# A transformer block on one core: modulation rows summed on VectorE, and part of the modulation moved to ScalarE

## The chip, the cores and the metric

The kernel runs on one core of one Trainium2 chip. The metric is the device time of one execution in microseconds. A core has five engines that run their own instruction queues in order and wait for one another on semaphores: TensorE (PE in the profile; its weight loads are listed as PEld), VectorE (DVE), ScalarE (ACT), GpSimd (POOL) and SyncE (SP), which here only issues DMAs. Before the change the median of three runs is 848.65 us (848.63 to 848.72).

## The reference

One block with a linear attention part and a gated feed-forward part, both steered by a condition vector `c`. Sequence length S = 2048, width D = 1024, hidden width F = 3584, 32 heads of 32 columns, bf16 inputs and output.

```python
mod = (silu(c) @ w_mod).reshape(1, 6, 1, -1)       # w_mod: 1024 x 6144
sa, ca, ga, sb, cb, gb = mod[:, 0], ..., mod[:, 5]  # six rows of 1024
h = layernorm(x) * (1 + ca) + sa
q, k, v = h @ wqkv
pq, pk = phi(q), phi(k)                             # phi(t) = where(t > 0, t + 1, exp(t)) + 1e-6
kv = sum over s of pk * v;  z = sum over s of pk    # per head
o = (pq @ kv) / (pq . z + 1e-6)
x = x + ga * (o @ wo)
h = layernorm(x) * (1 + cb) + sb
x = x + gb * ((silu(h @ w_gate) * (h @ w_up)) @ w_down)
```

The six rows of `mod` are vector-matrix products of length 1024. The rows sa and ca are needed at the start. The other four, ga, sb, cb and gb, are the "late" rows: ga scales the columns of the attention output, sb and cb shift and scale the second normalised input, gb scales the columns of the last product.

## The kernel before

**Tiles and stages.** The 2048 rows are 16 row tiles of 128, in four chunks of 512. `M4` holds h transposed, [128 partitions, chunk, 8 column blocks, 512 rows], so that a column block's sa, ca are one number per partition. The schedule is by hand: `seq` is a list of labelled pieces of TensorE work, and `put(label, ...)` hangs further work behind a label. The program is issued piece by piece in that order, and each engine keeps the order in which its instructions are issued.

The stages are, in order: K and V of chunk 0; then per chunk sc the stage KV (partial sums of kv, in banks 5 to 7 of PSUM, two halves of 16 products of 129 columns), with the next chunk's K (eight groups of eight 128x512 products, labels `("K", sc, 0..7)`) and V (eight groups, `("V", sc, 0..7)`) after it; Q of chunk 0 stands before K of chunk 1, and Q of chunks 1 to 3 after V of chunk 3; then the gate and up products (`("GU", sc, f)`, 28 per chunk) with the attention output products `o_mm` among those of chunk 0, and the down products (`D`). K, V, Q, gate and up groups write to one PSUM bank each, and take the banks 0 to 4 in rotation (`nextbank`).

**What the other engines do in these stages.** A K or Q group is evacuated by `phi_to`: an exponential on ScalarE (L237) and two instructions on VectorE (L238, L239). A V group is evacuated by a copy on ScalarE (L260). The layer norm of the next chunk's rows (`ln`) hangs behind K labels: statistics on VectorE (L196 to L200), three instructions on GpSimd (L202, L204, L211), and a DMA transpose into `M4`, issued on SP (L220). In chunk 1's K stage it normalises row tiles 8 to 11 (chunk 2), in chunk 2's K stage tiles 12 to 15 (chunk 3). `modulate` then applies `h * (1 + ca) + sa` in place on VectorE (L224), eight instructions per chunk, for chunks 2 and 3 behind `("V", sc, 4)` and `("V", sc, 6)` of the chunk before, for chunk 1 behind `("Q", 0, 2)` and `("Q", 0, 3)`.

**The late rows.** `load_late` brings half a row's columns, [128, 8, 512] bf16 (1 MB), into one of three slots `wml`: partition p holds the rows 8p to 8p + 7 of `w_mod`, and `scT` holds silu(c) in the same layout, [128, 8]. `late_mm` (L301) makes the product on TensorE with the weights as the stationary side: for each 128 columns eight products of one column each, 32 per half, 256 in all, into columns of bank 7 that the kv sums leave free. They hang behind the labels K and V, 2 and 6, of chunks 1 and 2. `late_fin` finishes sb and cb, or builds a repeated tile `rep` (L312), from which `late_bc` (L319) makes ga and gb as rows replicated over all partitions (`ga_bc`, `gb_bc`), eight products each, with two copies on ScalarE (L320). Late loads hang behind the same labels as `late_mm`, so they go out on SP among the transposes.

`wo` is loaded behind `("K", 2, 0)` and scaled by `ga_bc` on VectorE behind V of chunk 3 (L606). `kvz_build` (L282, L284) reads the kv sums behind `("KV", 3, 1)` and makes KVZ for the attention products `nd_mm`, the first of which is behind `("Q", 1, 3)`.

```python
    lab = [(k, sc, i) for sc in (1, 2) for k in ("K", "V") for i in (2, 6)]
    for i in range(8):
        put(lab[i], lambda i=i: late_mm(i))
        if i + 3 < 8:
            put(lab[i], lambda i=i: load_late(i + 3))
    put(("V", 1, 1), lambda: late_bc(2, ga_bc))
    put(("K", 2, 0), lambda: nc.sync.dma_start(out=wo, in_=wo_v))
    put(("K", 3, 1), lambda: late_bc(5, gb_bc))
```

## Time and profile before

| | |
|---|---|
| median of 3 runs | 848.65 us |
| profiled execution | 848.62 us, span 846.8 us |
| late products L301 | 256, 163 ns each in the profile |
| modulation by sa, ca on VectorE L224 | 34 instructions, mean 422 ns |
| wo scaling L606 | 8 instructions, mean 682 ns |
| wo load, issue to landing | 12.7 us |
| the five later late loads, issue to landing | 5.4 to 8.3 us |

The span is the time from the first to the last recorded instruction. Products on TensorE are pipelined: a 128x512 product is listed at 379 ns, while in a row of them one starts every 216 ns (eight in 1.73 us), so costs on TensorE are read from the distance of starts. Busy time by stretch, as the profile's windows of time give it (busy us of each engine):

| stretch, us | stage | PE | DVE | ACT | POOL |
|---|---|---|---|---|---|
| 64 to 80 | K of chunk 1 | 16.00 | 13.54 | 5.29 | 6.78 |
| 80 to 98 | V of chunk 1, KV | 17.01 | 4.84 | 5.85 | 2.48 |
| 98 to 115 | K of chunk 2, start of V | 17.00 | 14.19 | 4.77 | 6.95 |
| 115 to 132 | V of chunk 2, KV | 17.00 | 5.30 | 4.70 | 2.01 |
| 132 to 146 | K of chunk 3 | 14.00 | 8.60 | 5.73 | 0.00 |
| 146 to 162 | V of chunk 3, KV | 16.00 | 5.48 | 4.70 | 0.00 |

### The profile page before, as it was taken

The page shows a single profiled execution, that of the slowest core. Times are in us where ns is not written, and L with a number is a line of the kernel's source. Part 1 is how long each engine was busy: PE and PEld are TensorE (multiplying, and loading weights), DVE is VectorE, ACT ScalarE, POOL GpSimd, SP SyncE. Part 2 cuts the span into 40 slices and gives each one's busy share as a digit, 9 for nine tenths or more (in the row PEclk, how much of TensorE's full clock was granted, in tenths as well). Part 3 has the DMA queues.
Part 4 walks back from the last instruction along what each step waited for, and adds up shares of the span by engine and source line. Part 5 has one row for each costly group of instructions (what it writes and reads, how often), then busy time and mean ns, then how long its engine had stood idle before and what let it go on. Part 6 is the DMA issues. An engine that isn't in the chain of part 4 may idle for free.

```text
span 846.8 us, 10977 instructions
## 1 busy us (share of the span) xinstructions
PE 837.2 (99%) x4452; PEld 395.3 (47%) x4452; DVE 323.5 (38%) x617; ACT 143.9 (17%) x269; POOL 80.3 (9%) x143
## 2 busy tenths in 40 slices
PE   8999999999999999999999999999999999999998
PEld 4454555544444444444444444444444444444444
DVE  5757455497755655422111221221122122112222
ACT  3333233322311111111111001111000111100000
POOL 2124030014122323100000000000000000000000
PEclk9999999999999999999999999999999999999999
DMA  9984982045489987777875215555322555201220
GB/s 283 314 244 115 284 187 67 1 119 158 98 217 217 217 219 210 192 245 240 243 240 178 69 52 168 152 150 149 106 75 69 151 154 158 84 16 65 75 69 26
DMA packets 203763, 128.65 MB, mean 152 GB/s; under 512 B 50496, under 2 KB 189888, under 8 KB 203712
## 3 DMA queue, kind: packets, MB, share of 16 engines
q1 hardware_dynamic: 163008, 98.58, 40.8%
q10 hardware_dynamic: 38400, 20.98, 11.0%
q0 software_dynamic: 2304, 8.39, 2.6%
q8 instruction: 35, 0.57, 0.3%
q14 instruction: 16, 0.13, 0.1%
HBM read 103.81 MB, written 12.58 MB: 137 GB/s over the span
## 4 chain that ended last, share of the span: by engine, by line
PE 95%; SPq 2%; DVE 1%; DMA 1%; issue 0%; ACT 0%; DVEq 0%
PE bank L534 23%; PE bank L515 23%; PE bank L509 23%; PE bank L466 7%; PE bank L265 7%; PE bank L257 6%; PE bank L242 5%; DMA M<-in_w_mod_dram 1%; PE bank L439 1%; PE bank L274 1%; SPq L145 1%; SPq L142 1%; PE bank L301 1%; DVE stats L196 0%; DVE M L239 0%; DVE e L238 0%
## 5 line engine op out<-in xcount | busy, mean ns | idle before, releaser
L515 PE MATMUL bank<-M,M 128*128 128x512 bf16 x896 | 211.7, 379 | 0.0
L509 PE MATMUL bank<-M,M 128*128 128x512 bf16 x896 | 211.6, 379 | 0.0
L517 DVE TENSOR_TENSOR M<-bank,e 128x512 bf16<-128x512 f32 x112 | 77.4, 691 | 275.1 <-PE bank L515 274.0
L534 PE MATMUL bank<-M,M 128*128 128x512 bf16 (+1 forms) x700 | 147.9, 370 | 0.0
L512 ACT ACTIVATE e<-bank 128x512 f32<-128x512 f32 x112 | 66.8, 597 | 439.7 <-PE bank L509 414.4
L534 PEld LDWEIGHTS <-M 128*128 128x128 bf16 x924 | 90.4, 98 | 103.3
L515 PEld LDWEIGHTS <-M 128*128 128x128 bf16 x896 | 87.7, 98 | 105.7
L509 PEld LDWEIGHTS <-M 128*128 128x128 bf16 x896 | 87.3, 98 | 103.8
L538 DVE TENSOR_TENSOR M<-bank,gb_bc 128x512 f32<-128x512 f32 (+1 forms) x33 | 22.3, 675 | 149.2 <-PE bank L534 149.2
L242 PE MATMUL bank<-M,M 128*128 128x512 bf16 x256 | 58.3, 379 | 0.4 <-DVE M L334 0.3
L466 PE MATMUL bank<-M,M 128*128 128x512 bf16 x256 | 57.9, 379 | 0.0
L265 PE MATMUL bank<-M,M 128*128 128x512 bf16 x256 | 57.5, 379 | 0.0
L257 PE MATMUL bank<-M,M 128*128 128x512 bf16 x256 | 56.7, 379 | 0.0
L237 ACT ACTIVATE e<-bank 128x512 f32<-128x512 f32 x64 | 37.8, 598 | 100.0 <-PE bank L265 48.4
L534 PE MATMUL bank<-M 128*128 128x512 bf16 x224 | 51.0, 379 | 0.0
L239 DVE SCALAR_TENSOR_TENSOR M<-bank,e 128x512 bf16<-128x512 f32 x64 | 44.3, 691 | 3.7
L238 DVE TENSOR_SCALAR e<-e 128x512 f32<-128x512 f32 x64 | 27.8, 434 | 41.3 <-ACT e L237 41.3
L466 PEld LDWEIGHTS <-M 128*128 128x128 bf16 x256 | 25.0, 98 | 29.7
L257 PEld LDWEIGHTS <-M 128*128 128x128 bf16 x256 | 24.7, 98 | 29.0
L265 PEld LDWEIGHTS <-M 128*128 128x128 bf16 x256 | 24.6, 98 | 27.9
L242 PEld LDWEIGHTS <-M 128*128 128x128 bf16 x256 | 24.0, 97 | 28.1 <-DVE M L224 1.3
L468 DVE TENSOR_TENSOR M<-bank,M 128x512 f32<-128x512 f32 x32 | 22.1, 689 | 14.5 <-PE bank L466 14.3
(66 smaller groups left out, 334.1 us busy)
## 6 DMA issues: line engine op xcount, KB each, us to landing
M<-in_B_w_gate_dram SPq DMA_DIRECT2D x56, 512.0 KB, 3.9
M<-in_B_w_up_dram SPq DMA_DIRECT2D x56, 512.0 KB, 5.0
M<-in_w_mod_dram SPq DMA_DIRECT2D x8, 1024.0 KB, 6.6
x_scratch<-M POOLq DMA_DIRECT2D x16, 512.0 KB, 5.5
M<-x_scratch ACTq DMA_DIRECT2D x16, 512.0 KB, 3.4
M<-in_B_w_down_dram SPq DMA_DIRECT2D x6, 1024.0 KB, 8.1
M<-in_A_x_dram SPq DMA_DIRECT2D x16, 256.0 KB, 6.8
M<-in_w_mod_dram SPq DMA_DIRECT2D x8, 512.0 KB, 7.4
```

Of the source, the lines that this page charges most:

```text
L237: nc.scalar.activation(out=e[:], in_=acc, func=ACT.Exp)
L238: nc.vector.tensor_scalar(out=e[:], in0=e[:], scalar1=1.0, scalar2=PHI_EPS, op0=ALU.min, op1=ALU.add)
L239: nc.vector.scalar_tensor_tensor(out=dst, in0=acc, scalar=0.0, in1=e[:], op0=ALU.max, op1=ALU.add)
L242: nc.tensor.matmul(acc[:], lhsT=M4[:, sc_, cc, t * P:(t + 1) * P], rhs=wk[:, cc, h * NB:(h + 1) * NB], start=(cc == 0), stop=(cc == DC - 1))
L257: nc.tensor.matmul(acc[:], lhsT=M4[:, sc_, cc, t * P:(t + 1) * P], rhs=wv[:, cc, h * NB:(h + 1) * NB], start=(cc == 0), stop=(cc == DC - 1))
L265: nc.tensor.matmul(acc[:], lhsT=wq[:, cc, qc * P:(qc + 1) * P], rhs=M4[:, sc_, cc, :], start=(cc == 0), stop=(cc == DC - 1))
L466: nc.tensor.matmul(acc[:], lhsT=oTs[st % 3][:, cc, :], rhs=wo[:, cc, hs], start=(cc == 0), stop=(cc == DC - 1))
L509: nc.tensor.matmul(g_ps[:], lhsT=wg_blk[:, cc, fs], rhs=M4[:, sc_, cc, :], start=(cc == 0), stop=(cc == DC - 1))
L512: nc.scalar.activation(out=sg[:], in_=g_ps[:], func=ACT.Silu)
L515: nc.tensor.matmul(u_ps[:], lhsT=wu_blk[:, cc, fs], rhs=M4[:, sc_, cc, :], start=(cc == 0), stop=(cc == DC - 1))
L517: nc.vector.tensor_tensor(out=gus[sc_][:, f, :], in0=u_ps[:], in1=sg[:], op=ALU.mult)
L534: nc.tensor.matmul(y_ps[:, 0:w], lhsT=gus[sc_][:, f, t * P:(t + 1) * P], rhs=wd(f)[:, c0:c1], start=(f == 0), stop=(f == FC - 1))
```

## The change

Four things change together.

1. The late rows are no longer multiplied on TensorE. VectorE sums them per partition in float32: `late_sum` multiplies the first of the eight weight rows of a partition by its silu(c) value and adds the other seven one by one (`scalar_tensor_tensor`, each reading what the one before wrote). This makes a [128, 512] float32 tile whose sum over the partitions is the row. `late_split` writes its bf16 rounding ("high", on ScalarE) and the rest in bf16 ("low", on VectorE). The sum over partitions is a product with ones: `late_bc` for ga and gb (two 128x512 products, which also replicate the row), `late_cols` for sb and cb (eight products of one column per half, into bank 7). One row is worked on per V stage: ga in chunk 1, sb in chunk 2, cb in chunk 3, and gb in the gate and up products of chunk 1. Its two halves share one buffer `hlA`, as the three rows share `accA`.
2. The modulation of chunks 2 and 3 moves to ScalarE (`modulate_act`, with float32 copies of sa and 1 + ca in `modF`), two column blocks behind each of `("V", sc, 3)` to `("V", sc, 6)` of the chunk before. Chunk 1 stays on VectorE.
3. `wo` is scaled behind the K labels of chunk 3 instead of the V labels, and loaded behind `("K", 2, 3)` instead of `("K", 2, 0)`.
4. Late loads move: the second half of sb behind `("V", 1, 4)`, cb behind `("K", 2, 0)` and `("V", 2, 4)`, gb behind `("GU", 0, 20)`. The zero tile of the warm-up products moves into `M5`; `rep` goes, and the tiles `ones`, `scF` and `modF` come.

```diff
+    def modulate_act(sc_, cc):
+        h = M4[:, sc_, cc, :]
+        nc.scalar.activation(out=h, in_=h, func=ACT.Identity, scale=modF[:, 1, cc:cc + 1], bias=modF[:, 0, cc:cc + 1])
...
-    def late_mm(i):
-        q, kb = LATE[i // 2][0], i % 2
-        mps = bank[7][:, 320 + 8 * q:328 + 8 * q]
+    def late_sum(acc, kb, slot, js):
+        dst = acc[:, kb * NB:(kb + 1) * NB]
+        for j in js:
+            if j == 0:
+                nc.vector.tensor_scalar_mul(out=dst, in0=wml[slot][:, 0, :], scalar1=scF[:, 0:1])
+            else:
+                nc.vector.scalar_tensor_tensor(out=dst, in0=wml[slot][:, j, :], scalar=scF[:, j:j + 1], in1=dst,
+                                         op0=ALU.mult, op1=ALU.add)
+
+    def late_split(acc, kb, hl):
+        src = acc[:, kb * NB:(kb + 1) * NB]
+        nc.scalar.copy(out=hl[:, 0, :], in_=src)
+        nc.vector.tensor_tensor(out=hl[:, 1, :], in0=src, in1=hl[:, 0, :], op=ALU.subtract)
+
+    def late_cols(q, kb, hl):
+        o = 320 + 8 * q
         for ii in range(NB // P):
-            col = kb * (NB // P) + ii
-            for j in range(DC):
-                nc.tensor.matmul(mps[:, col:col + 1], lhsT=wml[i % 3][:, j, ii * P:(ii + 1) * P],
-                                 rhs=scT[:, j:j + 1], start=False, stop=(j == DC - 1), skip_group_check=True)
+            col = o + kb * (NB // P) + ii
+            for s_ in range(2):
+                nc.tensor.matmul(bank[7][:, col:col + 1], lhsT=hl[:, s_, ii * P:(ii + 1) * P], rhs=ones[:, 0:1],
+                                 start=False, stop=(s_ == 1), skip_group_check=True)
...
-    def late_bc(q, dst):
-        for h in range(NH):
-            b = nextbank()
-            for i in range(NB // P):
-                cc = h * (NB // P) + i
-                nc.tensor.matmul(b[:, i * P:(i + 1) * P], lhsT=rep[:, cc, :], rhs=ident[:], start=True, stop=True)
-            nc.scalar.copy(out=dst[:, h * NB:(h + 1) * NB], in_=b[:])
+    def late_bc(kb, hl, dst):
+        b = nextbank()
+        for s_ in range(2):
+            nc.tensor.matmul(b[:], lhsT=ones[:], rhs=hl[:, s_, :], start=(s_ == 0), stop=(s_ == 1))
+        nc.scalar.copy(out=dst[:, kb * NB:(kb + 1) * NB], in_=b[:])
...
     for sc in (2, 3):
         put_ln(sc, [("K", sc - 1, 1), ("K", sc - 1, 3), ("K", sc - 1, 5), ("K", sc - 1, 7),
-                    ("V", sc - 1, 4), ("V", sc - 1, 6)])
+                    ("V", sc - 1, 3), ("V", sc - 1, 4), ("V", sc - 1, 5), ("V", sc - 1, 6)])
...
-    for i in range(8):
-        put(lab[i], lambda i=i: late_mm(i))
-        if i + 3 < 8:
-            put(lab[i], lambda i=i: load_late(i + 3))
...
-    put(("K", 2, 0), lambda: nc.sync.dma_start(out=wo, in_=wo_v))
...
+    def sums(acc, kb, slot, labels):
+        for i, lab in enumerate(labels):
+            put(lab, lambda i=i: late_sum(acc, kb, slot, (2 * i, 2 * i + 1)))
+
+    put(("V", 0, 6), lambda: load_late(GA, 0, 0), lambda: load_late(GA, 1, 1), lambda: load_late(SB, 0, 2))
+    loads = {("V", 1, 4): [lambda: load_late(SB, 1, 0)], ("K", 2, 0): [lambda: load_late(CB, 0, 1)],
+             ("V", 2, 4): [lambda: load_late(CB, 1, 2)]}
+    for i, (q, sc) in enumerate(((GA, 1), (SB, 2), (CB, 3))):
+        for kb in range(2):
+            sums(accA, kb, (2 * i + kb) % 3, [("V", sc, 4 * kb + k) for k in range(4)])
+            nxt = ("V", sc, 4 + 4 * kb) if kb == 0 else (("K", sc + 1, 0) if sc < 3 else ("KV", 3, 0))
+            use = ("V", sc, 6) if kb == 0 else (("K", sc + 1, 2) if sc < 3 else ("Q", 1, 1))
+            put(nxt, lambda kb=kb: late_split(accA, kb, hlA))
+            put(use, (lambda kb=kb: late_bc(kb, hlA, ga_bc)) if q == GA else (lambda q=q, kb=kb: late_cols(q, kb, hlA)))
...
+    put(("K", 2, 3), lambda: nc.sync.dma_start(out=wo, in_=wo_v))
+    put(("GU", 0, 20), lambda: load_late(GB, 0, 0), lambda: load_late(GB, 1, 1))
+    for kb in range(2):
+        sums(accG, kb, kb, [("GU", 1, 5 * kb + i) for i in range(4)])
+        put(("GU", 1, 5 * kb + 4), lambda kb=kb: late_split(accG, kb, hlG))
+        put(("GU", 1, 5 * kb + 6), lambda kb=kb: late_bc(kb, hlG, gb_bc))
     for cc in range(DC):
-        put(("V", 3, cc), lambda cc=cc: nc.vector.tensor_tensor(out=wo[:, cc, :], in0=wo[:, cc, :], in1=ga_bc[:],
+        put(("K", 3, cc), lambda cc=cc: nc.vector.tensor_tensor(out=wo[:, cc, :], in0=wo[:, cc, :], in1=ga_bc[:],
                                                                op=ALU.mult))
```

## The prediction

> **What bounds the kernel now.** I read the page first, then the groups by line, then the timeline of each engine from 44 to 180 us, where the change works.

> ```profile
> PE 837.2 (99%) x4452; PEld 395.3 (47%) x4452; DVE 323.5 (38%) x617; ACT 143.9 (17%) x269; POOL 80.3 (9%) x143
> PE 95%; SPq 2%; DVE 1%; DMA 1%; issue 0%; ACT 0%; DVEq 0%
> ```

> Busy time and chain of waits: TensorE is the chain nearly throughout. Whatever leaves its queue shortens the run, and whatever makes its queue wait lengthens it. VectorE's 38% is an average; by stage it is another matter.

> ```profile
> 74.98 0.94 PE L301 MATMUL bank<-scT,M 128*128 128x1 bf16 x32
> 75.78 1.89 PE L242 MATMUL bank<-M,M 128*128 128x512 bf16 x8
> 77.51 3.62 PE L257 MATMUL bank<-M,M 128*128 128x512 bf16 x16
> 82.11 0.62 PE L319 MATMUL bank<-ident,rep 128*128 128x128 bf16 x8 [0.99 <-DVE rep L312]
> 82.57 1.89 PE L257 MATMUL bank<-M,M 128*128 128x512 bf16 x8
> ```

> Timeline of PE (start, length, what). By starts, 32 late products cost 75.78 - 74.98 = 0.80 us and a group of eight 128x512 products (77.51 - 75.78) 1.73. The ga broadcast starts 1.14 late (77.51 + 2 x 1.73 = 80.97) and takes 0.46.

> ```profile
> 79.68 1.27 DVE L196 BATCH_NORM_STATS2 stats<-M 128x6 f32<-128x512 bf16 x2
> 81.05 0.21 DVE L198 BATCH_NORM_AGGREGATE mv<-stats 128x2 f32<-128x12 f32 x1
> 81.30 0.15 DVE L200 TENSOR_SCALAR veps<-mv 128x1 f32<-128x1 f32 x1
> 81.37 0.69 DVE L312 COPY rep<-m 128x1024 bf16<-128x1024 bf16 x1
> 90.88 2.67 DVE L224 TENSOR_SCALAR M<-M,ca1T,saT 128x512 bf16<-128x512 bf16 x8 [8.83 <-DMA M<-M]
> 81.53 0.92 POOL L202 TENSOR_TENSOR rstd<-veps,neg_half 128x1 f32<-128x1 f32 x1 [1.43 <-DVE veps L200]
> 115.79 0.55 POOL L202 TENSOR_TENSOR rstd<-veps,neg_half 128x1 f32<-128x1 f32 x1 [1.43 <-DVE cb1T L310]
> 84.14 1.25 SPq L220 DMA_TRANSPOSE M<-M  x1
> ```
> ```profile
> DMA to landing us min/median/max: 3.1/3.2/6.7
> ```

> Timelines of DVE, POOL, SP, and the landing of the transposes (line 220). The modulation of chunk 2 cannot start before row tile 11 has gone through VectorE statistics, GpSimd normalisation and transpose. Here VectorE stood 8.83 us for it and nobody minded: the value copies of the V stage are on ScalarE.

> ```profile
> L214 ACT ACTIVATE M<-M,nmr,rstd 128x1024 bf16<-128x1024 bf16 x3 | 3.7, 1239 | 5.9 <-POOL nmr L204 5.9
> L260 ACT CAST M<-bank 128x512 bf16<-128x512 f32 x32 | 18.8, 586 | 38.9 <-PE bank L257 38.9
> L539 DVE TENSOR_TENSOR M<-M 128x512 bf16<-128x512 f32 (+1 forms) x33 | 22.3, 675 | 1.1
> L238 DVE TENSOR_SCALAR e<-e 128x512 f32<-128x512 f32 x64 | 27.8, 434 | 41.3 <-ACT e L237 41.3
> ```

> Groups: the nearest rows for the new operations.

> [...] the rstd of row tile 11 took 0.92 us beside the rep copy, 0.55 with VectorE idle.

> **The change, part by part.** "Label (V,1,3)" is the point after the fourth value group of chunk 1; times are on the clock of the trace before.

> *Removed from PE.* Eight times 0.80 = 6.4; two broadcasts 0.46 + 0.45; the 1.14 wait: 8.5 us. *Added to PE.* Four ones broadcasts of two 128x512 products, 4 x 0.43 = 1.7; four column sets of eight narrow products, 0.20 each (a quarter of the 0.80) = 0.8. Net -5.95 us if nothing waits.

> *New prices.* The sum step (line 312 of the new kernel) reads two SBUF streams in float32: nearest 691 ns (line 239) and 675 (539, whose full-width rows are 692). Each waits for the one before it; dependent pairs stand 0.03 apart (1.1 us over 33 at line 539): 0.725. A half is one scaling (434 ns by line 238) and seven steps: 5.5 us, sixteen instructions per V stage's two halves, 11 us of 13.8. It fits, tightly. ScalarE modulation of 128x512 with two pointer operands: [...] 0.81, every 0.72. Bounds for the pace 0.50 (as line 260's 586) and 0.80. The float32 high half on ScalarE: 0.61.

> *First stall, V stage of chunk 1.* Without late products K of chunk 1 ends at 62.09 + 8 x 1.73 = 75.9, and V group 6 at 88.0, where PE meets the first ones broadcast. Its input stands behind a chain:
> - VectorE was busy from 67.5 to 82.06 with 0.21 idle, so without late products it finishes the statistics of tile 11 only 0.3 earlier, 81.06.
> - GpSimd's three instructions then take 2.4 us to the transpose in the clean case (tile 15: 115.62 to 118.0), 2.8 beside the rep copy. [...] I take 3.3. Issue 84.35, landing +3.2 = 87.55; the 6.7 of before had a 1 MB load ahead and one behind, now gone.
> - ScalarE reaches this modulation after V copy 3, at 75.9 + 4 x 1.73 + 0.6 = 83.4, and waits, with value copies queued behind. From landing: two modulations, V copy 4, two modulations, the high half (label (V,1,4)), then VectorE's low half: 4 x 0.72 + 0.49 + 0.61 + 0.69 + hops of 0.05 = 4.8. PE resumes at 92.3 instead of 88.0: **4.3 us**.

> Five rotating banks hold V groups 4, 5, 6 meanwhile; no second stall adds. The last modulations and V copy 7 finish 0.9 before K of chunk 2 needs them.

> *Second stall, V stage of chunk 2.* Count from PE's resumption R. PE: broadcast, V 7, two KV halves (0.91), eight K groups, broadcast, seven V groups = R + 30.4 to the same point. VectorE, full all along: second half 5.5, eight phi pairs at 1.13, four statistics at 1.69, low half 0.72, one 0.7 wait for ScalarE = R + 22.8; GpSimd 3.3, landing 3.2, chain 4.8: R + 34.1. The wo load, now at label (K,2,3), is 2 MB queued ahead of transposes 14 and 15. Before, a transpose 2.4 us behind a 1 MB load landed 5.0 after issue, 1.0 after the load. From R + 18.7 I give the load 8 us, so it costs tile 15 about 0.3. **4.0 us**; 3.7 if wo costs nothing, 6.8 if it takes its 12.7 us of before (landing at R + 31.4, tile 15 a microsecond behind instead of at R + 29.3).

> *Third stall.* The last column set of cb, after Q group 1 of chunk 1, writes bank 7 columns, and its first product carries a wait on VectorE, behind the KVZ build that reads bank 7.

> ```profile
> 160.60 3.62 PE L265 MATMUL bank<-M,M 128*128 128x512 bf16 x16
> 163.01 0.15 DVE L284 TENSOR_TENSOR KVZ<-bank,mask 128x8 bf16<-128x8 f32 x1
> ```

> In this timeline of all engines the build ends at 163.16, Q group 1 at 160.60 + 1.73 = 162.33: **0.85 us**, up to 1.2 if VectorE enters Q late.

> *At nothing.* wo scaling in K of chunk 3: 8 x 0.61 + 8 x 1.13 = 13.9 beside 13.8 of PE; the lag of 2 us stays within five banks (6.9), then the last sums start late but end 2.6 before their use. Uncovered, the 4.9 would show. The gb sums: two steps and a product per 3.46 us gate/up group, 2.2 of VectorE; their 2 MB load goes out about 326 while the next weight load waits until 334. ones memset, scF and modF are single small instructions in idle time. Later ACT-queue DMAs keep their places.

> Sum: -5.95 + 4.3 + 4.0 + 0.85 = +3.2 us on the profiled execution's 848.62 (span 846.8 and 1.8 around it, 0.03 under the median): 851.8.

> **Rivals.**
> 1. *Faster: the removal wins.* If the modulation is in place before PE reaches the broadcasts, only -5.95 and 0.85 remain: 843.5. It decides when the stalls together stay under 4.25 us, that is tile 11 landing at about 85 rather than 87.55. For it: ScalarE is 17% busy. Against: the transposes cannot start earlier, VectorE being full before them.
> 2. *No change.* All three stalls at their cheap bounds (ScalarE pace 0.50, GpSimd 2.4, wo nothing): 2.5 + 1.9 + 0.85 = 5.25, so 847.9.
> 3. *The wo load holds the transposes.* Second stall 6.8 and, with slower GpSimd, 0.6 on both: 855.8. For it: the 6.7 us landing. Against: nothing else is queued then.

> **How the numbers follow.** Forecast 0.58; rival 1 0.10; rival 2 0.20; rival 3 0.12. A measurement can tell 0.2% (1.7 us) from no change. Faster 0.10, same 0.20, slower 0.70. The cheap bounds give 847.9, the dear ones 855.8; leaving out rival 1 and the tail of rival 3 gives 847.9 to 855.5.

> **What would show it.** Right: in chunks 1 and 2 ScalarE waits on a DMA before its modulation; PE shows idle of about 4 us before each first broadcast, released by VectorE's low half; 0.8 before the cb columns. Rows of line 312 at 0.69; modulation at 0.81; GpSimd rows longer beside the sums. Wrong: no idle at the broadcasts (rival 1), transposes 14 and 15 landing over 5 us after issue (rival 3), or PE waiting in K stages for VectorE's phi, which I cost at nothing.

## The result, and the profile after

The changed kernel takes 856.76 us (median of 4 runs, 856.41 to 857.3) against 848.64 (848.48 to 848.72, also 4): ratio 1.0096, 95% interval 1.0079 to 1.0114. Its span is 855.4 us against 846.8. It is slower, as forecast, but by 8.1 us and not by 3.2, outside the range.

From the page of the changed kernel, the busy times, the granted clock in 40 slices, and the chain that ended last:

```profile
PE 834.0 (98%) x4139; PEld 392.3 (46%) x4220; DVE 368.4 (43%) x670; ACT 159.2 (19%) x294; POOL 80.4 (9%) x144
PEclk9999898999999999999999999999999999999999
PE 90%; DVE 4%; SPq 2%; DMA 2%; issue 1%; ACT 1%; POOL 1%; DVEq 0%; ACTq 0%; POOLq 0%
```

TensorE's busy time fell by only 3.2 us, less than the removed work, and PE's share of the chain went from 95% to 90%: VectorE, ScalarE, DMAs and GpSimd are now links of it. The clock row has two digits 8, at slices 5 and 7, that is from 85 to 107 and from 128 to 150 us. Before, all forty were 9.

The timeline of PE in those two places (start, length, what, and in brackets the idle time ahead and what ended it):

```profile
75.48 12.25 PE L269 MATMUL bank<-M,M 128*128 128x512 bf16 x55
90.79 1.31 PE L338 MATMUL bank<-M,ones 128*128 128x512 bf16 x2 [3.06 <-ACT M L317]
...
97.04 1.90 PE L254 MATMUL bank<-M,M 128*128 128x512 bf16 x8
...
112.21 12.25 PE L269 MATMUL bank<-M,M 128*128 128x512 bf16 x55
127.83 0.18 PE L325 MATMUL bank<-ones,M 128*128 128x1 bf16 x1 [3.37 <-ACT M L317]
...
128.76 3.57 PE L269 MATMUL bank<-M,M 128*128 128x512 bf16 x8
...
133.86 2.05 PE L254 MATMUL bank<-M,M 128*128 128x512 bf16 x7
...
169.76 0.34 PE L325 MATMUL bank<-ones,M 128*128 128x1 bf16 x8 [1.37 <-DVE KVZ L296]
```

Seven V groups at 1.7275 us end at 75.48 + 12.09 = 87.57, so the first stall is 90.79 - 87.57 = 3.22 us. The second: 112.21 + 12.09 = 124.30 to 128.76, less 0.20 for the column products in it, is 4.26. The third is 1.37. That makes 8.85 us, where the prediction had 9.15.

What was missing is in the lengths. From the ones products at 90.79 to the K group at 97.04, TensorE does 0.43 + 1.73 + 0.91 = 3.07 us of work by the distances of starts of the kernel before, and takes 6.25. The windows of time of PE over that stretch (stretch, length, busy us, products, granted clock, DMA share, GB/s):

```profile
90.00:91.00 1.00, 0.21 (x1) 0.62 1.07 377
91.00:92.00 1.00, 0.86 (x3) 0.50 1.02 341
...
96.00:97.00 1.00, 1.00 (x12) 0.50 0.00 0
97.00:98.00 1.00, 1.00 (x8) 0.97 0.00 0
```

The granted clock is 0.50 from 90.2 (a mean of 0.62 over a microsecond is 0.76 of it at half) to 97.1. In the last microsecond of it no byte moves, so DMA traffic is not what slows the products. By the same reading it is 0.50 from 127.8 to 134.6. The price is 3.2 us in the first stretch (0.2 of it is a wait of the second ones product for the low half, which VectorE finishes at 91.46); in the second 5.10 - 2.64 = 2.5 for V group 7 and the KV halves, and 0.4 on the K group begun inside it: 6.0 together, rounded at the end. The ledger: -5.95 (removed and added work), -0.43 (K of chunk 1 ended earlier than I had counted: the first KV stage already begins at 46.04 here and at 46.46 before, a difference that I have not followed), +8.85, +6.0 makes +8.5, against a difference of spans of 8.6.

ScalarE's timeline at the two stalls shows the chain ahead of them:

```profile
86.82 1.52 ACT L237 ACTIVATE M<-M,modF 128x512 bf16<-128x512 bf16 x2 [3.60 <-DMA M<-M]
...
123.86 1.52 ACT L237 ACTIVATE M<-M,modF 128x512 bf16<-128x512 bf16 x2 [3.96 <-DMA M<-M]
```

ScalarE waits for the last row tile's transpose. Behind the modulations stand the V copies and the high half that the ones products need.

### The profile page after: what moved, and what is told of

Same layout as the page of the kernel before. It is cut to its first block, busy times and chain, and to the rows that moved or that the text cites. A ratio compares the mean times of both kernels' runs of the same rounds, so it can differ in the third digit from the quotient of the medians.

```text
span 855.4 us, 10476 instructions
## 1 busy us (share of the span) xinstructions
PE 834.0 (98%) x4139; PEld 392.3 (46%) x4220; DVE 368.4 (43%) x670; ACT 159.2 (19%) x294; POOL 80.4 (9%) x144
## 4 chain that ended last, share of the span: by engine, by line
PE 90%; DVE 4%; SPq 2%; DMA 2%; issue 1%; ACT 1%; POOL 1%; DVEq 0%; ACTq 0%; POOLq 0%
PE bank L553 23%; PE bank L534 23%; PE bank L528 22%; PE bank L485 6%; PE bank L277 6%; PE bank L254 4%; PE bank L269 3%; SPq L149 1%; DVE M L251 1%; PE bank L458 1%; SPq L146 1%; PE bank L286 1%; DVE stats L204 1%; DMA M<-in_w_mod_dram 1%; DMA M<-M 1%
## 5 line engine op out<-in xcount | busy, mean ns | idle before, releaser
L557 DVE TENSOR_TENSOR M<-bank,gb_bc 128x512 f32<-128x512 f32 (+1 forms) x33 | 22.3, 675 | 149.2 <-PE bank L553 149.2
L254 PEld LDWEIGHTS <-M 128*128 128x128 bf16 x256 | 24.5, 98 | 29.3 <-DVE M L232 1.3
L312 DVE SCALAR_TENSOR_TENSOR M<-M,scF,M 128x512 f32<-128x512 bf16 x42 | 33.2, 791 | 1.5
```

The lines of the kernel that those rows point to most:

```text
L254: nc.tensor.matmul(acc[:], lhsT=M4[:, sc_, cc, t * P:(t + 1) * P], rhs=wk[:, cc, h * NB:(h + 1) * NB], start=(cc == 0), stop=(cc == DC - 1))
L312: nc.vector.scalar_tensor_tensor(out=dst, in0=wml[slot][:, j, :], scalar=scF[:, j:j + 1], in1=dst, op0=ALU.mult, op1=ALU.add)
```

## The experiments

Ten kernels, in four groups. After the result my theory was: three stalls near the size forecast, and on top a clock of TensorE that falls to half when it stands idle for about 3 us. The 3 us were my estimate from the waits of the changed kernel: the clock fell to 0.50 with those of 3.22 and 4.26 us, and stayed at 1.00 with that of 1.37. Rivals: the slow products are held by DMA traffic or late operands; or the high/low chain itself costs the time and the moved modulation nothing.

**1. Is it the clock?** The two waits are filled with products that nobody reads: 14 products of 128x512 ahead of the first ones broadcast and 18 ahead of the first column set. The second variant has 5 and 5, leaving part of the idle time.

```diff
+    def fill(n):
+        b = bank[state["b"]]
+        for _ in range(n):
+            nc.tensor.matmul(b[:], lhsT=zt[:, 0:P], rhs=zt, start=True, stop=True)
...
             put(nxt, lambda kb=kb: late_split(accA, kb, hlA))
+            if kb == 0 and sc < 3:
+                put(use, lambda sc=sc: fill(14 if sc == 1 else 18))   # 5 and 5 in e2_fill5
```

> The changed kernel with 14 idle products (zero tile, result overwritten) ahead of the first ones broadcast of chunk 1 and 18 ahead of the first column set of chunk 2, so that TensorE works through its two long waits. Theory (the granted clock halves because TensorE stood idle for over 3 us, and costs about 6.0 us in the two stretches after the waits): both stretches run at clock 1.00, 856.8 - 6.0 = 850.8 us, between 849.5 and 852. Rival (the products after the waits are slow because of the DMA traffic or the freshly written operands beside them): no gain, 856 to 858 us.

> As the fill kernel with only 5 idle products (1.1 us) at each of the two places, so about 2.1 us of idle remain at the first and 3.2 us at the second. Theory with a limit near 3 us of idle: the first stretch keeps clock 1.00, the second is at the edge: 851 us if neither falls, 854 if only the second does. If any idle of over 1 us halves the clock: about 856.8 us.

Measured: full filling 852.27 us (852.03 to 852.62), ratio 1.0043 [1.0028, 1.0058]. More work on TensorE makes the kernel 4.5 us faster. PE's windows at the two places:

```profile
90.00:92.00 2.00, 1.60 (x8) 1.00 1.06 366
...
124.00:128.00 4.00, 3.62 (x25) 1.00 1.09 340
```

The clock stays at 1.00 with the same operands behind the filler and as much traffic (366 GB/s, against 377 and 341 in the changed kernel): the idle time caused the fall, and traffic and operands did not. The time is just above the range expected, 1.5 us above 850.8. Of this 0.45 lies ahead of the first wait (V group 6 ends at 88.02 instead of 87.57), and 0.5 is a wait of the second ones product for the low half (it starts at 91.98, the first at 91.25), which the 6.0 us had counted as won. Most of the rest is the difference between a profiled execution and a median: the two profiled ones, 857.3 and 852.37, differ by 4.9, the medians by 4.5.

Half filling: 855.38 us (852.8 to 855.63), ratio 1.0073 [1.0058, 1.0088]. It leaves idle times of 2.0 us and of 2.4 + 0.5. PE's windows after the first:

```profile
91.00:92.00 1.00, 0.69 (x2) 0.60 1.09 373
...
95.00:96.00 1.00, 1.00 (x18) 1.00 0.29 109
```

Half clock again, from 91.2 to 94.6 and from 128.8 to 132.2, 3.4 us each instead of 6.8. My limit of 3 us is refuted. One of the four executions took 852.8 at a mean clock of 0.998: with idle times of this size the fall comes in some executions and not in others.

**2. The same in the kernel before.** An idle time and nothing else: copies on GpSimd behind V group 6 of chunk 2, and one product that reads their output.

```diff
+    def pe_gap():
+        for _ in range(2):                                             # 5 in e8_gap5
+            nc.gpsimd.tensor_copy(out=scr, in_=v_c[:, 2, 4:8, 0:P])
+        nc.tensor.matmul(bank[state["b"]][:, 0:P], lhsT=scr[:, 0, :], rhs=scr[:, 0, :], start=True, stop=True)
+
+    put(("V", 2, 6), pe_gap)
```

> The kernel before with one product of TensorE behind V group 6 of chunk 2 that waits for two GpSimd copies of a V copy's result: an idle of about 1.9 us put into an otherwise unchanged kernel. Theory (limit near 3 us): clock 1.00 throughout, time + the idle, 850.5 us. If short idles halve the clock too: 853 us or more.

> As the gap kernel with five GpSimd copies: an idle of about 3.7 us. Theory: the clock halves about 3 us into the idle and stays so for some 6.6 us, which costs about 3 us beside the idle itself: 855.3 us. Rival (the slow stretch in the changed kernel has another cause): time + the idle alone, 852.3 us, clock 1.00.

Measured: with five copies 854.59 us (854.24 to 855.45) against 848.69, ratio 1.0071 [1.0056, 1.0086]. The line of PE's timeline that carries the wait, and then two of its windows of time:

```profile
129.33 0.29 PE L615 MATMUL bank<-M 128*128 128x128 bf16 x1 [3.67 <-POOL M L614]
```
```profile
130.00:132.00 2.00, 2.00 (x6) 0.50 1.04 252
...
132.00:134.00 2.00, 2.00 (x14) 0.50 0.02 6
```

The median loses 5.9 us. The profiled execution is the slowest of the four (855.45), and its span is 6.6 us longer: by the distances of starts 3.8 of it is the idle time (125.52 to 129.33), and 2.5 the half clock from 127.8 to 134.7, since V group 7 and one KV half take 5.1 us instead of 2.6. With two copies (wait 1.65 us) 852.39 us (850.77 to 852.78), ratio 1.0045 [1.0028, 1.0062]. The profiled execution, the 850.77, shows no half clock behind the wait and loses 2.1, near the wait alone; the other three lose 3.4 to 4.1. That would fit a fall in three of four, but those three have no profile, and their mean clocks (0.996 to 0.998) don't set them apart from the profiled one (0.998): it stays open.

**3. Which part makes the stalls?** The third stall alone (last column set behind Q group 2 instead of 1); the ones products of the first halves of ga and sb put off to K group 1 of the next chunk, with a second `hl` buffer; the changed kernel with the modulation back on VectorE; and the kernel before with the modulation on ScalarE and nothing else.

```diff
# e5_q12
-            use = ... else (("K", sc + 1, 2) if sc < 3 else ("Q", 1, 1))
+            use = ... else (("K", sc + 1, 2) if sc < 3 else ("Q", 1, 2))
# e6_use_late
-            use = ("V", sc, 6) if kb == 0 else ...
+            use = (("K", sc + 1, 1) if sc < 3 else ("V", sc, 6)) if kb == 0 else ...
-            put(nxt, lambda kb=kb: late_split(accA, kb, hlA))
+            put(nxt, lambda kb=kb: late_split(accA, kb, hlA2[kb]))
# e3_mod_dve
-        if sc_ == 1:
+        if sc_ >= 1:        # modulate, on VectorE, behind V 4 and V 6
# e4_mod_act, in the kernel before
+            for i in range(4):
+                put(labels[STC + i], lambda i=i: [modulate_act(sc_, cc) for cc in (2 * i, 2 * i + 1)])
```

> The changed kernel with the last column set of cb behind Q group 2 of chunk 1 instead of Q group 1. Theory (its only wait is for the KVZ build's read of bank 7, 1.37 us in the trace): that idle goes and nothing takes its place, 855.4 us. Rival (the attention products of the first row tile then wait for the columns' copy out of bank 7): 856.8 us, the wait moved to them.

> The changed kernel with two buffers for the high and low halves, and the products with ones for the first half of ga and sb behind K group 1 of the next chunk instead of V group 6. Theory (ScalarE's eight modulations after the transpose lands are what is late; the ones products are only the first to meet it): TensorE waits instead in K group 0 of the next chunk, 3.0 us and 3.5 us in short pieces, at full clock: 850 us (853 to 856 if the clock falls there too). Rival (the chain of high and low half alone is late): both waits go with their slow stretches, 843 to 845 us.

> The changed kernel with the modulation of chunks 2 and 3 back on VectorE at its labels of before; the rest as changed. Theory (the ScalarE modulation is most of the loss, the sums on VectorE alone would fit): the broadcasts find their halves in time, but VectorE's last four modulations stand behind half a sum and K group 0 waits for them about 2 to 3 us per chunk: 848 to 852 us. Rival (the sums on VectorE are the loss, wherever the modulation is): 855 us or more.

> The kernel before with the modulation of chunks 2 and 3 alone moved to ScalarE, at the labels of the change. Theory: ScalarE stands in its queue from V copy 3 until the transpose lands (90.9 in the trace before) and needs about 7.5 us for eight modulations and four copies, so K group 0 of the next chunk waits about 1.5 to 2.5 us per chunk; no wait is over 3 us in one piece, the clock stays: 850 to 854 us. Rival (ScalarE has room, nothing waits): 848.6 us.

Measured:

| | median, us (runs) | ratio to before, 95% |
|---|---|---|
| e5_q12 | 854.85 (4) | 1.0074 [1.0059, 1.0089] |
| e6_use_late | 854.72 (4) | 1.0077 [1.0060, 1.0094] |
| e3_mod_dve | 849.89 (18) | 1.0013 [1.0006, 1.0020] |
| e4_mod_act | 850.35 (17) | 1.0018 [1.0010, 1.0025] |

*e5_q12.* The third wait is gone from PE's waits. The gain over the changed kernel is 1.9 us, but its executions spread over 2 us (853.94 to 855.91). The profiled one, the fastest, has two half-clock stretches of 3.4 us where the profile of the changed kernel has two of 6.8, at places ahead of the edit. So how much of the gain is the 1.37 can't be read from it.

*e6_use_late.* If the high/low chain had been what was late, the stalls would have gone. They moved. PE's waits (engine, line, waited for: us in total, times, longest):

```profile
PE bank L255 <- ACT M L238: 4.6, 7, 1.3
```

TensorE now waits in the K groups of chunks 2 and 3, for the modulated columns themselves (line 238 is the modulation there). Behind the wait that the trace of the changed kernel names (the high half, line 317) stood the modulation, with 4.6 us left of about 7. The time lies in the range that I gave for a clock that falls there too, 853 to 856. In the profiled execution, the fastest of the four, it falls once, at 127.7, after waits of which none is listed at more than 1.3 us.

*e3_mod_dve and e4_mod_act.* The parts do not add. The moved modulation alone costs 1.7 us, everything else 1.2, both together 8.1. In e4 the clock is 1.00 in each window from 80 to 140 us. Its profile loses 1.0 us in K group 0 of chunk 2, which takes 2.7 us (95.48 to 98.18) instead of 1.73 while TensorE waits for the modulation on ScalarE, and nothing in chunk 3. The other 0.7 us is lost near 179, at the last attention products, where no modulation stands; ScalarE spends 3.34 us on the issue of a transpose just ahead of them (1.83 before), and I have not followed why. In e3 the waits at the V stages are at most 1.3 us each, the third stall stays (1.37), and VectorE does the modulation behind its sums, off ScalarE's queue. The profiled execution (850.02) has one stretch at half clock in these stages, from 122.5 to 125.9, after waits of 1.0 and 1.3 us with one product between. Its 18 runs range from 848.24, at the time of the kernel before, to 851.55. So without the moved modulation the removed TensorE work just pays for the waits, and the clock seems to decide on which side an execution ends: the five executions up to 848.68 have mean clocks of 0.997 to 1.0, the others 0.994 to 0.998. With it, the waits of VectorE's chain and of ScalarE's stand in one row and pass 3 us.

**4. A version without the waits.** Taken together: modulation on VectorE, in one piece behind V group 4 of the chunk before; one half of ga per V stage of chunks 1 and 2; sb by the narrow products of before; cb in chunk 3; gb as changed; `wo` scaled in V of chunk 3. The second variant puts cb's column sets later.

```diff
-                    ("V", sc - 1, 3), ("V", sc - 1, 4), ("V", sc - 1, 5), ("V", sc - 1, 6)])
+                    ("V", sc - 1, 4), ("V", sc - 1, 4)])
...
+    put(("K", 1, 4), lambda: late_mm(SB, 0, 2), lambda: load_late(SB, 1, 2))
+    put(("V", 1, 6), lambda: late_mm(SB, 1, 2))
+    sums(accA, 0, 0, [("V", 1, k) for k in range(4)])
+    put(("V", 1, 5), lambda: late_split(accA, 0, hlA))
+    put(("K", 2, 1), lambda: late_bc(0, hlA, ga_bc))
+    put(("K", 2, 0), lambda: load_late(CB, 0, 0), lambda: nc.sync.dma_start(out=wo, in_=wo_v))
+    sums(accA, 1, 1, [("V", 2, k) for k in range(4)])
+    put(("V", 2, 5), lambda: late_split(accA, 1, hlA))
+    put(("V", 2, 7), lambda: load_late(CB, 1, 1))
+    put(("K", 3, 1), lambda: late_bc(1, hlA, ga_bc))
+    sums(accA, 0, 0, [("K", 3, k) for k in (1, 3, 5, 7)])
+    put(("V", 3, 0), lambda: late_split(accA, 0, hlA))
+    put(("V", 3, 3), lambda: late_cols(CB, 0, hlA))       # ("V", 3, 6) in e10_hybrid2
+    sums(accA, 1, 1, [("V", 3, k) for k in range(4)])
+    put(("V", 3, 4), lambda: late_split(accA, 1, hlA))    # hlB in e10_hybrid2
+    put(("V", 3, 6), lambda: late_cols(CB, 1, hlA))       # ("Q", 1, 2), hlB
```

> A version from both: modulation on VectorE in one piece behind V group 4; ga by sums with one half per V stage (chunks 1 and 2), cb by sums in K and V of chunk 3 with wo scaled there as before, gb as changed; sb by narrow products as before; the products with ones where their inputs are long ready. TensorE loses 192 narrow products (4.8 us), two broadcasts (0.9) and the 1.1 us wait, and gains 1.7 + 0.4 us. Theory (sums fit where VectorE has room and no wait of TensorE stands behind them): 843.9 us, up to 846. Rival (VectorE falls behind in K and V of chunks 2 and 3 and TensorE waits for its evacuations): 849 us or more.

> The mixed version with its last two column sets of cb put where their input is long finished: the first half's after V group 6 of chunk 3 instead of group 3, the second half's after Q group 2 of chunk 1 instead of V group 6, from a buffer of its own. Theory (what the mixed version lost was 1.1 + 0.6 us of waiting of TensorE before the first of these sets and the clock fall of some executions after it): both waits go, no half-clock stretch between 145 and 160 us, and the time is the sum of what leaves TensorE alone: 848.6 - 4.75 = 843.9, allowed 843.5 to 844.8, without a second cluster of executions 1.8 us higher. Rival (the loss was elsewhere, in waits of TensorE for VectorE of some tenths that were spread over the stages): no change, 846 to 847, and two clusters as before.

Measured: e9_hybrid 846.5 us (845.97 to 848.0, 18 runs), ratio 0.9978 [0.9971, 0.9985]: faster than both kernels, but short of the 843.9 expected and just outside its range. Its executions stand in two clusters, eleven at 845.97 to 846.63 with mean clocks of 0.997 to 1.0, and seven at 847.51 to 848.0 with 0.995 or 0.996. The profiled one is of the second; PE's timeline has this line, and the clock is at 0.5 behind it, from 152.7 to 156.2:

```profile
150.96 0.18 PE L335 MATMUL bank<-ones,M 128*128 128x1 bf16 x1 [1.12 <-ACT M L317]
```

With the 0.55 that follows it, that is 1.7 us of idle. With the column sets put later, e10_hybrid2 takes 844.18 us (843.81 to 844.94, 5 runs) against 848.65, ratio 0.9949 [0.9935, 0.9963], in one cluster and in the range expected. The same products in PE's timeline now have no idle time ahead of them:

```profile
149.09 0.34 PE L336 MATMUL bank<-ones,M 128*128 128x1 bf16 x8
...
158.01 0.34 PE L336 MATMUL bank<-ones,M 128*128 128x1 bf16 x8
```

Two waits of 1.7 us in total were worth 2.3 us at the median. The sum of removed work, -4.75 us, now comes out at -4.5.

## Why the prediction was wrong in size

**The step that failed** is the last one, the sum "-5.95 + 4.3 + 4.0 + 0.85". It prices each stall at its length and lets TensorE go on at its old pace after it. In its place the traces show some 6.0 us lost behind the first two stalls, where the clock is at half, and e1_fill and e8_gap5 show that the idle time brings it on. With that term the prediction's own numbers give 851.8 + 6.0 = 857.8, against 857.3 for the profiled execution and 856.76 for the median. The trace of before could not show this term: its clock row has forty digits 9, and its longest wait of TensorE is 1.8 us (engine, line, waited for: us in total, times, longest):

```profile
PE bank L326 <- POOL M L211: 1.8, 1, 1.8
```

I had forecast two idle times of 4 us, over twice that, and took the pace after them from this trace.

**First stall (4.3 forecast, 3.22 measured).** VectorE's statistics ended at 80.63 (forecast 81.06) and the transpose went out at 83.78, 3.15 later (3.3). The modulation began at 86.82, 3.04 after issue (3.2). Up to TensorE 3.97 us passed where I had 4.8: I let the first ones product wait for the low half too, and it needs only the high one.

GpSimd's price, 3.3 by estimate, held. Its normalising instruction in the timeline, for row tile 10 and then for tile 11 beside the sums:

```profile
77.97 1.32 POOL L219 TENSOR_SCALAR M<-M,rstd,nmr 128x1024 bf16<-128x1024 bf16 x1
...
82.14 1.62 POOL L219 TENSOR_SCALAR M<-M,rstd,nmr 128x1024 bf16<-128x1024 bf16 x1
```

It and the two before it took 0.5 us more together: 0.71 + 0.42 + 1.62 for tile 11, 0.66 + 0.27 + 1.32 for tile 10. VectorE was at work beside both, with phi steps and statistics beside tile 10 and with the sum steps beside tile 11. So the longer times go with the sum steps; by what they hold GpSimd was not shown.

**Second stall (4.0, measured 4.26).** Right in size, and in this kernel partly by luck. Counted from the first ones product, V group 6 of chunk 2 ends after 33.5 us (forecast 30.4), since the half clock lies between, and VectorE's statistics end after 26.2 (22.8): VectorE was not "full all along", it stood idle for 3.05 us while the delayed K stage began. The two errors cancel. In e1_fill, at full clock, they end after 30.8 and 23.5, and the same stall, filler included, is 4.4, so the count itself was sound. The sign of rival 3 came half true: the `wo` load took 8.9 us (8 forecast), and the transpose of row tile 14 landed 7.2 us after issue. But tile 15, for which ScalarE waits 3.96 us, took 3.6, 0.5 more than the median of 3.1. With the rival's delay the stall would have been 6.8.

**Third stall (0.85, measured 1.37).** The place and the cause, the KVZ build, are right; VectorE came to it half a microsecond later than I took.

**Prices of the new operations.** The groups of VectorE and ScalarE:

```profile
L312 DVE SCALAR_TENSOR_TENSOR M<-M,scF,M 128x512 f32<-128x512 bf16 x42 | 33.2, 791 | 1.5
...
L237 ACT ACTIVATE M<-M,modF 128x512 bf16<-128x512 bf16 x16 | 12.2, 808 | 7.6 <-DMA M<-M 7.6
```

Modulation on ScalarE 808 ns (0.81 forecast, which no row of before shows), a pair in 1.52, so the second starts 0.71 after the first (0.72). The sum step is dearer than I took: 791 ns, seven in a row in 5.47 us without GpSimd beside them (0.78 a step against 0.725), and 6.29 with it. For the first stall that was without weight, since the transpose was later still.

**At nothing.** The `wo` scaling in K of chunk 3 and the sums of gb stayed hidden: no wait of TensorE at either place.

**Rivals.** Rival 1 (843.5) had about the right sum for a version without stalls: e10_hybrid2 is close to it at 844.18, but its parts are others. Rival 2 is refuted by the stalls, rival 3 by the 4.26.

## What to carry to other kernels

Waits of TensorE from 2.0 us (e2_fill5) to 3.67 (e8_gap5) as the profiles list them, and pairs of shorter ones close together (1.0 + 1.3 us in e3_mod_dve, 1.1 + 0.55 in e9_hybrid), were followed by a stretch at clock 0.50. A wait of this size is priced at its length plus what the half clock takes afterwards: half of a stretch of 3.4 or 6.8 us, here up to about 3 us each. Products that do nothing were cheaper than such waits (852.27 us in e1_fill against 856.76). When an operation is moved to an engine that looks idle, ask what stands behind it in that engine's queue and for what it waits itself: here ScalarE was 17% busy, and yet it put the copies and the high half behind a DMA. Two changes that cost 1 to 2 us apart can cost 8 together, when their waits add up to one long one.

## What the runs showed of the hardware

```profile
86.82:90.23 3.41, 0.91 (x5) 1.00 0.40 111
90.23:97.06 6.83, 5.91 (x26) 0.50 0.72 252
97.06:127.78 30.72, 27.24 (x137) 1.00 0.57 164
...
121.83:125.25 3.42, 1.57 (x8) 1.00 0.47 122
125.25:128.66 3.41, 1.08 (x12) 1.00 1.09 346
```

- What goes with a fall is the idle time within the one step that ends at it, in one piece or several. By the distances of starts it is 2.7 us ahead of the first fall of the change. In e5_q12 it is 2.0 us in the first step shown, which no fall follows, and 2.5 in the second, which one does. Over all twelve profiles, their first microseconds included, it is 1.9 to 3.4 us ahead of each of the 18 falls before the last product, and at most 2.0 us in every step at full clock that no fall follows. A few products are missing from the traces, so these figures hold to some 0.2 us. The line lies near 2 us of idle time in a step; this is read from the profiles afterwards, and no run was made to test it.
- By this reading it depends on where an idle time lies on the grid whether the clock falls, and how soon: 2.2 us after the idle time began at the first wait of e2_fill5, 4.4 us at its second, and in e9_hybrid at 152.7, with products running again from 151.7 on. The grid lies differently in the profiles: its first line behind the start of the span is at 1.5 us in the changed kernel, at 2.5 in e2_fill5 and at 3.0 in e3_mod_dve. That executions of one kernel differ by 2 us for this reason is my guess and was not shown, since one execution of each was profiled.
- The half-clock stretches in these stages are 3.4 us long (e2_fill5, e3_mod_dve, e5_q12, e6_use_late, e9_hybrid) or 6.8 (both of the change, e8_gap5), one step or two.
